# Transposes of q, k and normalised tokens moved from TensorE to the DMA, in a fused window attention and MLP kernel

## The chip, the cores and the metric

One core of one Trainium2 chip. The metric is the device time of one execution in microseconds (us). A kernel is run several times and its median is given; lower is better. Each comparison uses runs of both kernels from the same session on the same chip.

## The reference, cut to what matters

```python
# q, k, v: (4, 8, 768, 64) float32; n_sink = 4, window = 128
scores = q @ k.transpose(0, 1, 3, 2) / sqrt(64)
keep = is_sink | in_window            # 4 sink columns, and the last 128 positions
a = softmax(where(keep, scores, -1e9))
x = heads_merged(a @ v)               # (4, 768, 512)
xn = (x - mean) / sqrt(var + 1e-6) * g_ln
out = x + relu(xn @ w_ch1) @ w_ch2    # 512 -> 2048 -> 512
```

A tile is 128 positions of one batch with all heads: 24 tiles, 6 for each batch. The scores need q and k with the head dimension on the partitions, and the up-projection needs the tokens with the model dimension on the partitions. So both have to be transposed.

## The kernel before

A small planner in the kernel orders the operations: each has a cost on an engine, and the emitted program is the order in which the planner would start them. In the kernel before, TensorE transposes q and k, and VectorE or ScalarE fetch the result out of PSUM:

```python
def prep(b, c, hp, key):              # one head pair of one batch
    ...
    for x in range(2):                # q, k
        for r in range(e):
            for h2 in range(2):
                nc.tensor.transpose(pb.t[64 * h2:64 * (h2 + 1), x, 128 * r:128 * (r + 1)],
                                    qn[(b, x)].t[:, c, 2 * hp + h2, D * r:D * (r + 1)], ident)
    ...                               # copy(eng, kb.t[...], pb.t[...]) on VectorE or ScalarE
```

For each tile the attention result is centred, transposed on TensorE, and fetched with the LN weight:

```python
ENG[e].tensor_scalar(xnb[t].t, xf, mvb[g][:, ti, 0:1], None, op0=ALU.subtract)
...
for j in range(NDM):
    nc.tensor.transpose(pt.t[:, 128 * j:128 * (j + 1)], xnb[t].t[:, 128 * j:128 * (j + 1)], ident)
...
nc.vector.tensor_tensor(xtb[g].t[...], pt.t[...], gt.unsqueeze(2).to_broadcast(...), op=ALU.mult)
```

The attention of batch b+1 is woven into the MLP of batch b, so TensorE always has matmuls to do, as long as the data of batch b+1 is there in time.

Names in the views below: qkn is q and k as loaded, qkt the same transposed; xn is a tile's normalised tokens, xnt the same transposed; vn is v; pm, pw and bank are PSUM buffers. The sink scores are those against the 4 sink columns. A narrow up-matmul is one of 256 columns; the others have 512.

The softmax here doesn't subtract the row's maximum and nothing guards it: scores larger than these inputs give would overflow.

Of the kernel before, what the change touches and what calls it, by code (L numbers as in the profile page):

```python
# [31 lines left out]
class Plan:  # L32
# [4 lines left out]
    LAT = {"PE": 0.2, "ACT": 0.1, "DVE": 0.1, "POOL": 0.15, "DMA": 2.0, "SP": 0.1}  # L37
    SLACK = {"PE": 0.15}
# [15 lines left out]
    def emit(self):  # L54
# [3 lines left out]
        def ready(o):  # L58

            r, held = 0.0, False  # L60
            for d in o.deps:
                if d.end is None:
                    return None, False
                r = max(r, d.end)
            n = {}
            for b in o.alloc:
                h = hist.get(b.pool, [])
                k = n[b.pool] = n.get(b.pool, -1) + 1
                if len(h) + k >= b.bufs:
                    for u in h[k - b.bufs].users:  # L70
                        if u.end is not None:
                            r = max(r, u.end)
                        elif b.pool == "pw":
                            held = True
                        else:
                            return None, False
            return (None if held else r), held

        trace = []
        while waiting:  # L80
# [29 lines left out]
            o.end = s + c + self.LAT[e]  # L110
# [10 lines left out]
def kernel(  # L121
# [12 lines left out]
    nc = tc.nc  # L134
# [67 lines left out]
    LEAD = 24.0  # L202
# [24 lines left out]
    gt = consts.tile([128, NDM], FP32)  # L227
    nc.scalar.dma_start(gt, moe_g_ln.rearrange("(j p) -> p j", p=128))
# [34 lines left out]

    nc.vector.memset(neg_half, -0.5)
# [11 lines left out]
    chunks_of = {b: 2 if b == 0 else 1 for b in range(B)}  # L276

    qn, loaded = {}, {}

    def load_qk(b, c, x, h0, h1, key, deps=()):  # L280
        n = chunks_of[b]
        w = S // n
        alloc = []
        if (b, x) not in qn:
            qn[(b, x)] = Buf("qkn", 4)
            alloc = [qn[(b, x)]]
        qb = qn[(b, x)]

        def go(_):
            if qb.t is None:  # L290
                qb.t = qkn.tile([128, n, H, w // 128 * D], BF16, name="qkn")
            nc.gpsimd.dma_start(qb.t[:, c, h0:h1], (q, k)[x][b, h0:h1, c * w:(c + 1) * w, :]  # L292
                                .rearrange("h (p r) d -> p h (r d)", p=128))

        o = op({"POOL": 0.6 + 0.04 * (h1 - h0)}, go, [begun] + list(deps), key, alloc, [qb])
        o = op({"DMA": (h1 - h0) * w * 256 / 390e3}, None, [o], key)
        for h in range(h0, h1):
            loaded[(b, c, x, h)] = o
        return o
# [3 lines left out]
    def load_v(b, r, key, deps=()):  # L303
        def go(_):
            nc.gpsimd.dma_start(vn_buf[b % 2][:, r, :, 0:D],  # L305
                                v[b, :, 128 * r:128 * (r + 1), :].rearrange("h p d -> p h d"))

        before = [vread[(b - 2, i)] for i in (r, r + 1) if (b - 2, i) in vread] + [vs_done.get(b - 2)]
        o = op({"POOL": 0.9}, go, [begun] + list(deps) + before, key)
        vcast[(b, r)] = op({"DMA": 1.15}, None, [o], key)  # L310
        return o
# [5 lines left out]
    def load_w(which, c, after, key):  # L317
# [8 lines left out]
        o = op({"POOL": 0.9}, go, after, key)  # L326
        w_in[(which, c)] = op({"DMA": 2.65}, None, [o], key)
        return o

    op({"DMA": 1.4}, None, (), -1000)  # L330
    for half in range(2):
        for x in range(2):
            load_qk(0, 0, x, 4 * half, 4 * half + 4, -500 + half)
    for r in range(2):
        load_v(0, r, -486 + r)
    for x in range(2):
        load_qk(0, 1, x, 0, H, -491 + x)
    wi = begun
    w_key = [-460, -452, -450, -448]
    for r in range(2, RB):  # L340
        load_v(0, r, -470 + 5 * r)
    for c in range(4):
        wi = load_w(1, c, [wi], w_key[c])
    for c in range(W2_FIRST):
        wi = load_w(2, c, [wi, w_in.get((1, c))], -440 + c)
    for x in range(2):
        wi = load_qk(1, 0, x, 0, H, -436 + x, [wi, w_in[(1, 2 + x)]])
    for c in range(W2_FIRST, 4):
        wi = load_w(2, c, [wi, w_in[(2, 0)]], -434 + c)
    for r in range(RB):  # L350
        load_v(1, r, -430 + r, [loaded[(1, 0, 0, 0)]])
# [4 lines left out]
    def prep(b, c, hp, key):  # L356

        n = chunks_of[b]
        e = S // (128 * n)
        w = 128 * e  # L360
        alloc = []
        if b not in kqb:
            kqb[b] = Buf("qkt", 2)
            alloc = [kqb[b]]
        kb = kqb[b]
        pb = Buf("pm", 3) if n > 1 else Buf("pw", 2)

        def go(_):
            if kb.t is None:
                kb.t = qkt.tile([128, 2, HP, S], BF16, name="qkt")  # L370
            if n > 1:
                pb.t = ps_m.tile([128, 512], FP32, name="pm").bitcast(BF16)[:, 0:2 * w]
                pb.t = pb.t.rearrange("d (x m) -> d x m", x=2)
            else:
                pb.t = ps_w.tile([128, 2, 512], FP32, name="pw").rearrange("d x m -> d (x m)").bitcast(BF16)
                pb.t = pb.t.rearrange("d (x m) -> d x m", x=2)
            for x in range(2):
                for r in range(e):
                    for h2 in range(2):
                        nc.tensor.transpose(pb.t[64 * h2:64 * (h2 + 1), x, 128 * r:128 * (r + 1)],  # L380
                                            qn[(b, x)].t[:, c, 2 * hp + h2, D * r:D * (r + 1)], ident)

        deps = [ident_done] + [loaded[(b, c, x, h)] for x in range(2) for h in (2 * hp, 2 * hp + 1)]
        o0 = op({"PE": 0.12 * e + 0.2}, go, deps, key, alloc + [pb], [kb] + [qn[(b, x)] for x in range(2)])
        for xs in ([(0, 1)] if n > 1 else [(0,), (1,)]):
            def back(eng, x0=xs[0], x1=xs[-1] + 1):
                copy(eng, kb.t[:, x0:x1, hp, c * w:(c + 1) * w].rearrange("d x (p r) -> d x p r", r=e),
                     pb.t[:, x0:x1, 0:w].rearrange("d x (r p) -> d x p r", r=e))

            m = len(xs) * w  # L390
            o = op({"DVE": 0.18 + m * 0.00101, "ACT": 0.16 + m * 0.00084}, back, [o0], key, (), [pb, kb])
            for x in xs:
                prepped[(b, c, hp, x)] = o

    def ready(b, hps, lo, hi):
        n = chunks_of[b]
        w = S // n
        return [prepped[(b, c, hp, x)] for c in range(n) for hp in hps for x in range(2)
                if c * w < hi and (c + 1) * w > lo]
# [3 lines left out]
    def sinks(b, key):  # L403
# [37 lines left out]
        o1 = op({"DVE": 0.2}, mul_k, ready(b, range(HP), 0, S) + [sunk.get(b - 2), sinks_done], key, (), [kb])  # L441
        ov = op({"PE": 0.22}, mm_v, [vcast[(b, 0)], sinks_done, ones_done], key, [vb])
        vs_done[b] = op({"DVE": 0.7}, mul_v, [ov, vread.get((b - 2, RB - 1))], key, (), [vb])
        o2 = op({"PE": 0.4}, mm, [o1], key, [pb], [kb])
# [4 lines left out]
    def scores(t, halves, key):  # L449
# [32 lines left out]
        o0 = op({"PE": cost}, mm, ready(b, hps, 128 * r, 128 * r + n) + [neg_done, edone.get((t - 1, 1)) if last else None], key, pbs + ebs, [kb])  # L482
# [38 lines left out]
    def values(t, key):  # L521
# [58 lines left out]
        def cen(e):  # L580
            xf = xb[t].t.rearrange("p h d -> p (h d)")
            xnb[t].t = xnpool.tile([128, DM], BF16, name="xn")
            ENG[e].tensor_scalar(xnb[t].t, xf, mvb[g][:, ti, 0:1], None, op0=ALU.subtract)
# [4 lines left out]
        o = op({"DVE": 0.42}, cen, [o], key, [xnb[t]], [xb[t]])  # L588
# [11 lines left out]
        pt = Buf("pt", 1)  # L600
        alloc = [pt]
# [4 lines left out]
        def tr(_):  # L606
            if xtb[g].t is None:
                xtb[g].t = xtpool.tile([128, NDM, 512], BF16, name="xnt")
            pt.t = pt_view
# [3 lines left out]
        def back(_):  # L613
            nc.vector.tensor_tensor(xtb[g].t[:, :, 128 * ti:128 * (ti + 1)],  # L614
                                    pt.t[:, 0:512].rearrange("p (j c) -> p j c", j=NDM),
                                    gt.unsqueeze(2).to_broadcast([128, NDM, 128]), op=ALU.mult)

        o = op({"PE": 0.24}, tr, [o], key, alloc, [xnb[t]] + ([] if ti == 0 else [xtb[g]]))
        turned[t] = op({"DVE": 0.69}, back, [o], key, (), [pt, xtb[g]])
# [33 lines left out]
    def down(g, ti, quarter, key):  # L653
# [18 lines left out]
        if quarter == 3:  # L672
# [13 lines left out]
            op({"DMA": 0.8}, put, [o], -300 + key, (), [ob])  # L686
# [10 lines left out]

    for b in range(B):
        k0 = bkey[b]
        if b == 0:  # L700
            for c in range(2):
                for hp in range(HP):
                    prep(0, c, hp, k0 + (0.6 if c else -40) + 0.1 * hp)
# [17 lines left out]
        if b > 1:  # L721
            for x in range(2):
                load_qk(b, 0, x, 0, H, k0 - 60 + x, [vcast[(b - 1, RB - 1)]])
            for r in range(RB):
                load_v(b, r, k0 - 50 + r, [loaded[(b, 0, 0, 0)]])
        for hp in range(HP):
            prep(b, 0, hp, k0 - 12 + 3 * hp)
# [53 lines left out]
```

## Time and profile before

| | before |
|---|---|
| median of 3 runs | 240.51 us (240.5 to 240.91) |
| span of the profiled run | 239.2 us |
| TensorE busy | 228.8 us (96%) |

The lines on which the prediction rests are in the prediction. Its rows of digits cut the span into 40 equal slices, a digit being the busy share of a slice in tenths (9 is 90% or more). One view is added here. It cuts the run into stretches; the columns are the length, TensorE's busy time (number of instructions), the granted TensorE clock (1 is full), the DMA share (above 1 where the two DMA queues overlap) and GB/s. Kernel before:

```profile
core 0: us, PE busy (x), PEclk, DMA share, GB/s
20.00:50.00 30.00, 29.43 (x328) 1.00 1.51 188
50.00:80.00 30.00, 29.76 (x313) 1.00 0.96 132
80.00:110.00 30.00, 29.35 (x317) 1.00 0.84 98
110.00:140.00 30.00, 29.76 (x290) 1.00 0.10 36
140.00:170.00 30.00, 30.00 (x209) 1.00 0.10 36
```

After 20 us TensorE is never idle for as much as 0.7 us in 30, at full clock.

### The profile page before, as it was taken

What the parts mean: (1) busy time and instruction counts of PE and PEld (TensorE: products, weight loads), DVE (VectorE), ACT (ScalarE), POOL (GpSimd) and SP (SyncE); (2) the same over time, 40 slices, a digit from 0 to 9 for tenths busy, and PEclk for the clock granted to TensorE, in tenths of its full rate; (3) what the DMA queues carried; (4) which work ended last, traced back from release to release, by engine and by line L of the source; (5) the groups of instructions that cost most, each with busy time, mean ns of one, the idle gap of its engine ahead of it and who ended that gap; (6) DMA issues with size and microseconds to landing.
All of it is one profiled execution on the core that took longest, in us unless ns stands there. A gap on an engine that the chain in (4) does not pass through costs nothing.

```text
span 239.2 us, 4785 instructions
## 1 busy us (share of the span) xinstructions
PE 228.8 (96%) x2051; PEld 130.3 (54%) x2051; DVE 119.6 (50%) x231; ACT 121.1 (51%) x193; POOL 59.3 (25%) x86
## 2 busy tenths in 40 slices
PE   7779999999999989999999999999999999999993
PEld 7344788874545654545545544455445455444850
DVE  0247973026798587766766745666204664021002
ACT  2678768865451668862157580706730455500810
POOL 8965448800460922240000200200000211000000
PEclk9999999999999999999999999999999999999999
DMA  6999999999295499200111000211002110001202
GB/s 69 160 182 194 198 207 175 178 188 205 59 162 105 84 202 183 18 3 13 75 47 44 4 0 3 88 44 47 0 1 88 47 44 0 3 22 65 90 0 88
DMA packets 43622, 20.23 MB, mean 85 GB/s; under 512 B 30289, under 2 KB 40529, under 8 KB 43601
## 3 DMA queue, kind: packets, MB, share of 16 engines
q0 software_dynamic: 39616, 13.63, 50.6%
q1 hardware_dynamic: 3456, 6.29, 7.1%
q8 instruction: 16, 0.26, 0.4%
q10 hardware_dynamic: 528, 0.00, 0.1%
q14 instruction: 6, 0.04, 0.1%
HBM read 27.27 MB, written 6.29 MB: 140 GB/s over the span
## 4 chain that ended last, share of the span: by engine, by line
PE 85%; DVE 6%; DMA 4%; POOL 2%; ACT 1%; issue 1%; POOLq 0%
PE pm L665 34%; PE pm L634 34%; PE pw L475 4%; DMA qkn<-in_k_dram 4%; PE pw L380 3%; PE bank L611 3%; PE pw L542 2%; DVE xt L569 2%; POOL qkn L292 2%; PE pw L545 2%; DVE qkt L183 2%; PE pw L535 1%; ACT qkt L181 1%; DVE st L575 1%; PE pw L471 1%
## 5 line engine op out<-in xcount | busy, mean ns | idle before, releaser
L634 PE MATMUL pm<-xnt,w1s 128*128 128x256 bf16 (+1 forms) x512 | 89.9, 326 | 0.0
L486 ACT ACTIVATE e<-pw 128x1024 bf16<-128x1024 f32 x44 | 43.7, 1023 | 49.8 <-PE pw L475 49.6
L634 PEld LDWEIGHTS <-w1s 128*128 128x128 bf16 x512 | 48.0, 98 | 29.6 <-issue 1.5
L665 PE MATMUL pm<-w2s,h1t 128*128 128x512 bf16 x256 | 58.9, 379 | 0.0
L643 ACT ACTIVATE h1t<-pm 128x512 bf16<-128x512 f32 x60 | 35.9, 598 | 25.5 <-PE pm L634 25.1
L678 DVE SCALAR_TENSOR_TENSOR ot<-pm,rs,xt 128x512 f32<-128x512 f32 x24 | 18.0, 750 | 45.7 <-PE pm L665 45.5
L665 PEld LDWEIGHTS <-h1t 128*128 128x128 bf16 x256 | 24.1, 98 | 28.1 <-issue 1.1
L643 ACT ACTIVATE h1n<-pm 128x256 bf16<-128x256 f32 x63 | 24.0, 384 | 18.7 <-PE pm L634 15.8
L665 PE MATMUL pm<-w2s,h1n 128*128 128x512 bf16 x128 | 30.1, 379 | 0.0
L594 POOL TENSOR_SCALAR ve<-mv 128x2 f32<-128x2 f32 (+1 forms) x8 | 2.4, 305 | 82.6 <-DVE mv L578 82.1
L305 POOL DMA_DIRECT2D vn<-in_v_dram x24 | 21.2, 906 | 5.8 <-PE pw L545 4.7
L183 DVE COPY qkt<-pw 128x768 bf16<-128x768 bf16 x10 | 9.6, 958 | 21.6 <-ACT qkt L181 21.2
L614 DVE TENSOR_TENSOR xnt<-bank,gt 128x512 bf16<-128x512 bf16 x24 | 16.4, 685 | 7.5 <-PE bank L611 7.3
L665 PEld LDWEIGHTS <-h1n 128*128 128x128 bf16 x128 | 11.6, 98 | 12.5 <-issue 0.6
L498 POOL TENSOR_SCALAR_AFFINE_SELECT e<-e 128x512 bf16<-128x512 bf16 (+1 forms) x8 | 6.1, 759 | 49.6 <-ACT e L486 49.6
L496 DVE TENSOR_TENSOR e<-e,mask 128x1024 bf16<-128x1024 bf16 x22 | 15.0, 687 | 5.8 <-ACT e L486 5.6
L569 DVE TENSOR_TENSOR xt<-pw,rc 128x512 bf16<-128x512 f32 x24 | 16.6, 691 | 0.8
L575 DVE BATCH_NORM_STATS2 st<-xt 128x6 f32<-128x512 bf16 x24 | 16.5, 690 | 0.5
L380 PEld LDWEIGHTS <-qkn 128*64 128x64 bf16 x384 | 11.4, 109 | 8.9 <-issue 3.6
L542 PE MATMUL pw<-vn,e 128*128 128x65 bf16 x192 | 15.8, 193 | 0.0
L542 PEld LDWEIGHTS <-e 128*128 128x128 bf16 x192 | 13.7, 98 | 2.7 <-DMA vn<-in_v_dram 0.2
L475 PE MATMUL pw<-qkt 64*128 64x256 bf16 (+1 forms) x192 | 14.8, 263 | 0.2 <-DVE qkt L183 0.2
(55 smaller groups left out, 179.4 us busy)
## 6 DMA issues: line engine op xcount, KB each, us to landing
out_dram<-ot SPq DMA_DIRECT2D x24, 256.0 KB, 2.0
vn<-in_v_dram POOLq DMA_DIRECT2D x24, 128.0 KB, 8.2
qkn<-in_q_dram POOLq DMA_DIRECT2D x3, 768.0 KB, 10.9
qkn<-in_k_dram POOLq DMA_DIRECT2D x3, 768.0 KB, 12.4
w1s<-in_moe_w_ch_dram POOLq DMA_DIRECT2D x4, 512.0 KB, 11.7
w2s<-in_moe_w_ch_dram POOLq DMA_DIRECT2D x4, 512.0 KB, 11.4
qkn<-in_q_dram POOLq DMA_DIRECT2D x2, 192.0 KB, 4.5
qkn<-in_k_dram POOLq DMA_DIRECT2D x2, 192.0 KB, 4.6
```

What stands on the lines that cost most here:

```text
L305: nc.gpsimd.dma_start(vn_buf[b % 2][:, r, :, 0:D], v[b, :, 128 * r:128 * (r + 1), :].rearrange("h p d -> p h d"))
L380: nc.tensor.transpose(pb.t[64 * h2:64 * (h2 + 1), x, 128 * r:128 * (r + 1)], qn[(b, x)].t[:, c, 2 * hp + h2, D * r:D * (r + 1)], ident)
L475: nc.tensor.matmul(pb.t[:, h2, i], lhsT=kb.t[64 * h2:64 * (h2 + 1), 1, hp, 128 * r:128 * (r + 1)], rhs=kb.t[64 * h2:64 * (h2 + 1), 0, hp, ...
L486: nc.scalar.activation(eb.t, pb.t, AF.Exp, scale=scale)
L542: nc.tensor.matmul(pv[:, half, hh, :], lhsT=weights_of(t, half, i, h2, 0), rhs=vn[:, r, h, 0:D + 1], start=fresh and hh == 0, stop=(r == 0 ...
L569: nc.vector.tensor_tensor(xb[t].t.rearrange("p (a h) d -> p a h d", a=2), pv[:, :, :, 0:D], rc[0].unsqueeze(3).to_broadcast([128, 2, 4, D] ...
L575: nc.vector.bn_stats(st, xf)
L614: nc.vector.tensor_tensor(xtb[g].t[:, :, 128 * ti:128 * (ti + 1)], pt.t[:, 0:512].rearrange("p (j c) -> p j c", j=NDM), gt.unsqueeze(2).to ...
L634: nc.tensor.matmul(pb.t[:, 0:n], lhsT=w1s[:, j, 128 * ht:128 * (ht + 1)], rhs=xtb[g].t[:, j, 0:n], start=(j == 0), stop=(j == NDM - 1))
L643: nc.scalar.activation(hb.t[:, 0:n], pb.t[:, 0:n], AF.Relu)
L665: nc.tensor.matmul(pb.t, lhsT=h1b[(g, ht)].t[:, 128 * ti:128 * (ti + 1)], rhs=w2s[:, ht, :], start=(ht == 0), stop=(ht == NH1 - 1))
L678: nc.vector.scalar_tensor_tensor(ob.t, in0=pb.t, scalar=rsb[g][:, ti:ti + 1], in1=xb[t].t.rearrange("p h d -> p (h d)"), op0=ALU.mult, op1 ...
```

## The change

The intent: take the transposes off the engine that is the bound. q and k of batches 1 to 3 come in small loads (128 positions, all heads) and each is turned by one DMA transpose issued by SyncE. The tokens of batches 1 to 3 are turned by a DMA transpose too. The call for such a transpose takes no weight, so the LN weight goes into the centring, as one VectorE instruction with two operations ("the fold" below). Core of the diff, cuts marked:

```diff
-                        nc.tensor.transpose(pb.t[64 * h2:64 * (h2 + 1), x, 128 * r:128 * (r + 1)],
-                                            qn[(b, x)].t[:, c, 2 * hp + h2, D * r:D * (r + 1)], ident)
...
+            nc.gpsimd.dma_start(dst[:, r], (q, k)[x][b, :, 128 * r:128 * (r + 1), :].rearrange("h p d -> p h d"))
...
+            nc.sync.dma_start_transpose(kb.t[:, x, :, 128 * r:128 * (r + 1)], qb.t[:, H * D * r:H * D * (r + 1)])
+        o = op({"SP": 0.75}, go, [lo], key, alloc, [kb, qb])
+        prepped[(b, r, x)] = op({"XD": 0.7}, None, [o], key, (), [kb, qb])
...
-            ENG[e].tensor_scalar(xnb[t].t, xf, mvb[g][:, ti, 0:1], None, op0=ALU.subtract)
+            nc.vector.scalar_tensor_tensor(xnb[t].t, in0=xf, scalar=mvb[g][:, ti, 0:1], in1=gb,
+                                           op0=ALU.subtract, op1=ALU.mult)
...
+        if b > 0:
+            o = op({"SP": 0.75}, lambda _: nc.sync.dma_start_transpose(room(), xnb[t].t), [o], key, alloc, ...)
+            turned[t] = op({"XD": 0.7}, None, [o], key, (), [xnb[t], xtb[g]])
+            return
```

The two `op` lines: the planner takes a transpose to cost SyncE 0.75 us and to land 0.7 + 2.0 us after that, on a resource "XD" of its own. The rest of the diff spreads the LN weight over the partitions with one matmul, limits the loads in flight to seven, puts the loads in another order, and changes some planner settings (slack per engine; the lead of a batch's attention, 24 to 30).

## The prediction

> **What bounds the kernel now**
>
> I read the page first (busy times, slices), then the chain in order of time, then short windows of the DMA.
>
> ```profile
> PE 228.8 (96%) x2051; PEld 130.3 (54%) x2051; DVE 119.6 (50%) x231; ACT 121.1 (51%) x193; POOL 59.3 (25%) x86
> ...
> PE   7779999999999989999999999999999999999993
> ...
> DMA  6999999999295499200111000211002110001202
> ...
> PE 85%; DVE 6%; DMA 4%; POOL 2%; ACT 1%; issue 1%; POOLq 0%
> ```
>
> TensorE is busy 96% of 239.2 us and makes up 85% of the chain; VectorE and ScalarE stand at half. A busy TensorE need not be at its peak, so I look at the chain in order of time:
>
> ```profile
> 37.81 12.31 PE pm L634 x112
> 50.13 0.79 PE pw L380 x24
> 50.92 0.97 PE pm L665 x4
> 51.89 0.81 PE pw L380 x24
> ...
> 67.58 0.33 PE bank L611 x4
> 67.91 1.73 PE pm L665 x8
> 69.64 0.22 PE bank L611 x4
> ...
> 228.14 6.92 PE pm L665 x32
> 235.09 0.75 DVE ot L678
> ```
>
> Eight 512-column matmuls take 1.73 us, 216 ns each, in an unbroken stream: the MLP is at its rate, and each instruction among it costs its own time. The reader sees what the q/k transposes (24 per head pair) cost there, 0.79 to 0.86 us a group, and what the four token transposes of a tile cost, 0.22 us (0.33 us in some places). Four matmuls after a q/k group take 0.97 us in place of 0.86. So whatever leaves TensorE after about 15 us should shorten the run, unless a wait takes its place. TensorE's idle time there is small: from the windows 50 to 80, 80 to 122 and 122 to 166 us, 30 - 29.76, 42 - 41.35 and 44 - 43.76, together 1.1 us, mostly at the q/k transposes, whose results VectorE and ScalarE have to fetch out of PSUM.
>
> The other resource that is full is DMA, up to about 60 us: its row reads 9 for nine slices, at 160 to 207 GB/s. Small-row loads run slower than large-row ones:
>
> ```profile
> 92.00:93.00 1.00, 1.00 (x10) 0.53 (x9) 0.07 (x1) 1.00 (x2) 0.00 (x0) 1.00 2.50 152
> ```
>
> ```profile
> vn<-in_v_dram POOLq DMA_DIRECT2D x24, 128.0 KB, 8.2
> out_dram<-ot SPq DMA_DIRECT2D x24, 256.0 KB, 2.0
> ```
>
> The window is a microsecond with only v loads (last column GB/s): 152, so a 128 KB load takes some 0.85 us. In the page's DMA issues the last column is issue to landing; the last line's is a store's, 2.0 us in the median.
>
> **What the Trainium skill says**
>
> - VectorE: DVE Perf Modes, section "The three transpose paths": a 128x128 bf16 transpose takes 390 ns on TensorE and 1309 ns through the DMA crossbar, which lands in SBUF. Those are single times; in this trace four on TensorE occupy 0.22 us, because they are pipelined. No run before has the DMA path.
> - DMA: Bandwidth & Descriptors, section "Latency and other measured facts": the DMA transpose was measured at 261 GB/s, about 350 to 400 if contiguous. A 128x512 bf16 tile is 131 KB, so I estimate 0.5 us of transfer for each. This trace can't confirm it.
> - The same page, "Issuing engines are not separate DMA queues": all issuers share 16 DMA engines and interleave. The trace agrees: a store lands in 2.0 us alone, but in up to 5.8 us (the tile view's longest) while loads are in flight.
> - TensorEngine Tiling (Array Packing), section "Key Properties": changing the tiling mode drains TensorE. That agrees with 0.97 for 0.86 us after a group that writes 64-wide column tiles: 0.11 us for each such group.
>
> **The change part by part**
>
> *Removed from TensorE.* Batches 1 to 3 have 4 head pairs each, 12 groups of 24 transposes: 12 x 0.81 = 9.7 us. Their mode switches: 12 x 0.11 = 1.3 us. The token transposes of 18 tiles: 18 x 0.22 = 4.0 us. The idle gaps that the fetches out of PSUM and the LN chain made between 50 and 166 us: up to 1.1 us. All of it lies in the stretch in which TensorE is the bound. Sum 16.1 us.
>
> *Removed from the other engines.* 14 fetches on ScalarE (799 ns) and 10 on VectorE (958 ns), 11.2 and 9.6 us; and 24 weighted fetches of tokens on VectorE, 685 ns, 16.4 us. Six plain copies stay for batch 0, five of them on ScalarE in the new order. Off the path, worth nothing by itself; it only leaves VectorE more slack.
>
> *Added.* The centring becomes a scalar_tensor_tensor with the weight: 402 ns become some 750 (the output's instruction of that kind and size took 750), 24 x 0.35 = 8.4 us on VectorE, less than the 26 it loses. One fp32 matmul that spreads the LN weight, before the first q/k has landed (14.7 us for the last of batch 0), so hidden.
>
> *DMA.* 54 transposes on SyncE's queue, 54 x 0.5 = 27 us of DMA time by the estimate. The q and k loads of batches 1 to 3 become 36 loads of 128 KB in the form of v's: 12 x 0.85 = 10.2 us a batch, against 1.57 MB at about 205 GB/s = 7.7 us. From 60 us on, DMA is mostly idle and this is hidden. In the first 60 us it is not.
>
> *Where it can bite: batch 1.* In the new instruction order the first scores of batch 1 stand after 120 of the 192 narrow up-matmuls of batch 0; before, its q/k transposes stood after all 192 (at 50.13 us). 72 x 0.108 us = 7.8 us earlier: TensorE gets there at about 42.4 us. Loads ahead of it are 6.0 MB, and slices 1 to 6 of the page carry (69 + 160 + 182 + 194 + 198 + 207) x 5.98 us = 6.0 MB, so they end at about 36 us; the trace has the third w2 load landing at 37.6. The scores need three small loads: 37.6 + 3 x 0.85 = 40.2, then a transpose of 2 us alone, up to 4 beside loads: 42 to 44 us. A stall of 0 to 2 us. Next the sink scores of batch 1, about 13 us of TensorE work later by the counts in the order and the times above, at 55.5 to 56 us. They need all of q: the fifteenth small load, one w2 load of 2.6 us and ten transposes before it: 37.6 + 15 x 0.85 + 2.6 + 10 x 0.5 = 58, plus 2 us to land = 60 us. A stall of some 4 us, which contains the first one. TensorE runs in order and nothing after makes it good.
>
> *Later batches* are loaded right behind batch 1, long before their scores (80 us and 120 us). Tokens have time too: the shortest way from the last values of a group to its first up-matmul is about 11 us of TensorE work in the new order, against some 2.5 us on VectorE and 3 to 5 for the transfer.
>
> Sum: 240.5 - 16.1 + 4.0 = 228.4 us.
>
> **Rivals**
>
> 1. *All hidden.* The transposes are short and land before TensorE asks: 240.5 - 16.1 = 224.4. For it: the loads and transposes are issued in small pieces, and the planner's modelled latencies are generous. Against it: DMA is already full when batch 1 is wanted, and the order brings it forward by 8 us.
> 2. *DMA transposes are far slower than a copy.* If each 128x128 block took the page's single 1309 ns in turn, 54 x 4 x 1.3 = 281 us would be more than the whole run, and DMA would become the bound, at 280 us or more. Against it: 16 engines share the work, the same skill gives 261 GB/s[...]. At half the estimated rate (1 us each) the batch 1 stall grows by 5 us: 233.
> 3. *SyncE's queue blocks.* It is in order and mixes q/k transposes, token transposes and stores. In the new order a token transpose of the first tile of batch 1 stands before the last two q/k transposes of that batch: it waits for scores, values and LN of that tile, at about 53 us. That is earlier than q's last load, so it should add nothing; if the scores slip by 4 us, it slips too and could add 1 to 3 us: 230 to 231.
> 4. *VectorE becomes the bound.* Against it: it is busy 50% now and loses more than it gains.
>
> **Range and chances**
>
> Between no stall (224.4) and a stall of 10 us (234), with a little for a better start (less VectorE work for each tile of batch 0): 223.5 to 234, and 228.4 as the middle. Faster by over 2% means under 235.7; that needs under 11.3 us of new stalls. 0.90 for it. Within 2%: 0.06. Slower: 0.04, which is rival 2.
>
> **What will show it**
>
> TensorE's busy time should fall by about 15 us to 213 or 214; the groups of q/k transposes should keep only batch 0 (96 matmuls) and the token transposes only 24. The waits of TensorE should name the DMA of the transposed q/k at batch 1, once or twice, some 4 us in all between 42 and 62 us, and nearly none after. The DMA view should show transposes landing in 2 to 3 us when loads are quiet and in 4 us or more before 60 us. I am wrong if TensorE waits for transposed q/k in batches 2 and 3 or for transposed tokens, if transposes take over 1 us of DMA time each, if SyncE's order holds up batch 1 longer than its loads do, or if TensorE's busy time falls by much less than 15 us.

## The result

| | before | after |
|---|---|---|
| median | 240.71 us (240.5 to 244.23, 4 runs) | 249.65 us (248.44 to 250.01, 4 runs) |
| ratio of fast runs | 1 | 1.0366, 95% interval 1.032 to 1.0411 |
| span of the profiled run | 239.2 us | 248.3 us |
| mean granted clock | 1.000 | 0.950 |

Ratios here and below are the mean time of one kernel's fast runs over that of the other's fast runs of the same rounds, so not quite the ratio of the medians that are quoted (before's 244.23, over 1.5% above its fastest, is not in it). The change made the kernel 3.7% slower; 228.4 us was predicted. The results are correct.

The page of the kernel after, the lines that answer to those shown of before:

```profile
PE 222.6 (90%) x1670; PEld 121.5 (49%) x1690; DVE 109.3 (44%) x207; ACT 110.8 (45%) x178; POOL 87.9 (35%) x115
...
PE   6978999379749999839999999999999999999993
...
PEclk9979999959968999968999999999999999999999
DMA  6999999999992999999947990122101231012102
...
PE 71%; DMA 19%; POOL 3%; DVE 2%; SPq 1%; issue 1%; ACT 0%; POOLq 0%; DVEq 0%
```

TensorE's row has three holes (slices 8, 12 and 18, of 6.2 us each), where it had none. The clock row dips at or behind each hole. DMA, which before had little to do from slice 17 on, is busy to slice 24 but for slices 13, 21 and 22, and makes 19% of the chain that ends last, where it made 4%. The same stretches as above, kernel after:

```profile
20.00:50.00 30.00, 24.43 (x282) 0.99 1.66 177
50.00:80.00 30.00, 24.00 (x181) 0.78 1.54 137
80.00:110.00 30.00, 24.77 (x207) 0.96 1.63 161
110.00:140.00 30.00, 29.84 (x200) 0.93 1.31 129
140.00:170.00 30.00, 29.78 (x205) 1.00 0.67 94
```

From 140 us on both kernels are alike. All is lost before. What TensorE waited for, kernel after (us in total, times, longest):

```profile
PE pm L446 <- DMA qkt<-qkn: 9.7, 2, 4.9
PE pw L487 <- DMA qkt<-qkn: 5.1, 1, 5.1
```

And where, from the timeline of the kernel after (start, length, what, and in brackets the idle time before it):

```profile
50.98 1.04 PE L487 MATMUL pw<-qkt 64*128 64x256 bf16 x8 [5.07 <-DMA qkt<-qkn]
...
71.62 0.62 PE L446 MATMUL pm<-qkt,ks 128*32 128x512 bf16 x4 [4.82 <-DMA qkt<-qkn]
72.17 4.74 PE L686 MATMUL pm<-w2s,h1n 128*128 128x512 bf16 x11
...
109.58 0.62 PE L446 MATMUL pm<-qkt,ks 128*32 128x512 bf16 x4 [4.91 <-DMA qkt<-qkn]
```

The first is the first scores of batch 1, the second its sink scores (which need all of q), the last the sink scores of batch 2. Together 5.07 + 4.82 + 4.91 = 14.8 us. The third line shows what follows a wait: eleven 512-column matmuls in 4.74 us, some 430 ns each, where 216 was the rate. The clock records say the same; the stretches of half clock in the kernel after, with TensorE's busy time in them:

```profile
15.20:18.60 3.40, 3.14 (x32) 0.50 1.57 192
49.33:56.16 6.83, 5.18 (x28) 0.50 1.93 151
69.81:76.64 6.83, 5.02 (x15) 0.50 0.90 147
107.36:114.18 6.82, 4.60 (x20) 0.50 1.99 156
```

Half of that busy time is lost: 17.9 / 2 = 9.0 us. (The first stretch lies in the start-up and occurs in some of the profiled runs here and not in others.) With this the books close. Work taken off TensorE, at full clock: 228.8 - (222.6 - 9.0) = 15.2 us. Idle time: 248.3 - 222.6 = 25.7 us, where before had 239.2 - 228.8 = 10.4, so 15.3 us more. 239.2 - 15.2 + 15.3 + 9.0 = 248.3. These are books, not yet causes: a part of them that is taken away may come back elsewhere, and the experiments show that it does.

Why did the transposes come late? Kernel after, the tile view of the transposed q and k: first the issue on SyncE (shortest, median and longest in ns), then the us from issue to landing:

```profile
L399 SPq DMA_TRANSPOSE qkt<-qkn x36: 1189/1252/3184, 38.6 to 146.0; - x36
...
DMA to landing us min/median/max: 2.4/7.4/9.4
```

A transpose lands 2.4 us after its issue when DMA is quiet and 7 to 9 us after it beside loads. It keeps SyncE for 1.25 us in the median, not 0.75. What one costs the DMA itself shows in a window with one token transpose alone (154 to 158 us), beside one with a store of 256 KB alone (226 to 230 us):

```profile
154.00:158.00 4.00, 4.00 (x26) 1.00 0.16 33
226.00:230.00 4.00, 4.00 (x20) 1.00 0.17 66
```

0.16 x 4 = 0.64 us for 33 x 4 = 132 KB: 206 GB/s. A transposed byte costs the DMA nearly twice what a stored one does (0.17 x 4 = 0.68 us for 264 KB).

Batch 2 was late for a further reason. GpSimd issues the loads, in order, and it stood at the window mask of a tile whose scores waited for batch 1. GpSimd's timeline, kernel after:

```profile
79.50 0.64 POOL L510 TENSOR_SCALAR_AFFINE_SELECT e<-e 128x512 bf16<-128x512 bf16 x1 [17.07 <-ACT e L498]
```

DMA worked off what was in flight until some 74 us and was nearly idle for the last 6 of these 17 us (slice 13 of its row, 2), and the loads of batch 2's later tiles came out at 81 us and after. Whether this made the third wait is tested in experiment 4. The last q transpose that its sink scores need was issued at 101.8 us and landed at 109.5.

### The profile page after: what moved, and what is told of

Read it like the earlier page. It is cut to its first block, busy times and chain, and to the rows that moved or that the text cites. A ratio compares the mean times of both kernels' runs of the same rounds, so it can differ in the third digit from the quotient of the medians.

```text
span 248.3 us, 4183 instructions
## 1 busy us (share of the span) xinstructions
PE 222.6 (90%) x1670; PEld 121.5 (49%) x1690; DVE 109.3 (44%) x207; ACT 110.8 (45%) x178; POOL 87.9 (35%) x115
## 3 DMA queue, kind: packets, MB, share of 16 engines
q0 software_dynamic: 70816, 13.64, 67.5%
## 4 chain that ended last, share of the span: by engine, by line
PE 71%; DMA 19%; POOL 3%; DVE 2%; SPq 1%; issue 1%; ACT 0%; POOLq 0%; DVEq 0%
PE pm L686 33%; PE pm L655 29%; DMA qkt<-qkn 10%; DMA qkn<-in_q_dram 5%; PE pw L487 4%; DMA qkn<-in_k_dram 4%; PE pw L554 2%; POOL qkn L310 2%; PE pw L557 1%; SPq L399 1%; PE pw L547 1%; PE pm L446 1%; DVE xt L581 1%; DVE st L587 1%; PE pw L483 0%
## 5 line engine op out<-in xcount | busy, mean ns | idle before, releaser
L655 PE MATMUL pm<-xnt,w1s 128*128 128x256 bf16 (+1 forms) x505 | 91.1, 334 | 0.4
L655 PEld LDWEIGHTS <-w1s 128*128 128x128 bf16 x512 | 50.1, 101 | 35.6 <-issue 4.5
L686 PE MATMUL pm<-w2s,h1t 128*128 128x512 bf16 x249 | 56.9, 379 | 0.4
L699 DVE SCALAR_TENSOR_TENSOR ot<-pm,rs,xt 128x512 f32<-128x512 f32 x24 | 18.0, 749 | 68.1 <-PE pm L686 50.9
L664 ACT ACTIVATE h1n<-pm 128x256 bf16<-128x256 f32 x56 | 20.9, 386 | 20.0 <-PE pm L655 17.7
L510 POOL TENSOR_SCALAR_AFFINE_SELECT e<-e 128x512 bf16<-128x512 bf16 (+1 forms) x7 | 4.9, 704 | 63.8 <-ACT e L498 63.8
L607 POOL TENSOR_SCALAR ve<-mv 128x2 f32<-128x2 f32 (+1 forms) x8 | 5.3, 668 | 38.8 <-DVE mv L590 38.6
L508 DVE TENSOR_TENSOR e<-e,mask 128x1024 bf16<-128x1024 bf16 x23 | 16.4, 720 | 5.5 <-ACT e L498 5.2
L595 DVE SCALAR_TENSOR_TENSOR xn<-xt,mv,gb 128x512 bf16<-128x512 bf16 x24 | 18.3, 767 | 0.8
L325 POOL DMA_DIRECT2D qkn<-in_k_dram x18 | 16.1, 895 | 6.0 <-DMA w2s<-in_moe_w_ch_dram 1.9
L325 POOL DMA_DIRECT2D qkn<-in_q_dram x18 | 16.4, 908 | 1.1 <-PE pm L655 0.5
```

What stands on the lines that cost most here:

```text
L325: nc.gpsimd.dma_start(dst[:, r], (q, k)[x][b, :, 128 * r:128 * (r + 1), :].rearrange("h p d -> p h d"))
L595: nc.vector.scalar_tensor_tensor(xnb[t].t, in0=xf, scalar=mvb[g][:, ti, 0:1], in1=gb, op0=ALU.subtract, op1=ALU.mult)
L655: nc.tensor.matmul(pb.t[:, 0:n], lhsT=w1s[:, j, 128 * ht:128 * (ht + 1)], rhs=xtb[g].t[:, j, 0:n], start=(j == 0), stop=(j == NDM - 1))
L664: nc.scalar.activation(hb.t[:, 0:n], pb.t[:, 0:n], AF.Relu)
L686: nc.tensor.matmul(pb.t, lhsT=h1b[(g, ht)].t[:, 128 * ti:128 * (ti + 1)], rhs=w2s[:, ht, :], start=(ht == 0), stop=(ht == NH1 - 1))
L699: nc.vector.scalar_tensor_tensor(ob.t, in0=pb.t, scalar=rsb[g][:, ti:ti + 1], in1=xb[t].t.rearrange("p h d -> p (h d)"), op0=ALU.mult, op1 ...
```

## The experiments

First theory: three late landings of transposes, made by a DMA that is full, cost the time, and the half clock behind each adds to it. Rivals: the half clock alone makes the loss; the planner's wrong costs made a bad order, which a better order would mend; the parts that seemed harmless (fold of the LN weight, token transposes) cost. All kernels gave correct results. Each line of numbers is the median, the range and the ratio to before of its own session (the medians of before lay between 240.77 and 241.93).

### 1. Spins at the three waits

The kernel after with junk matmuls ahead of the three groups.

```diff
+            for _ in range(getattr(o, "fill", 0)):
+                self.spin()
+        o2.fill = 80 if b in (1, 2) else 0       # sink scores
+        o0.fill = 80 if t in (6,) else 0         # first scores of batch 1
```

> The changed kernel with 80 junk matmuls (about 55 ns each, 4.4 us in all) put on TensorE ahead of each of the three groups at which it stood idle for some 5 us: the first scores of batch 1 and the sink scores of batches 1 and 2. Theory A (TensorE waits for transposed q and k, and each wait of 5 us is followed by some 5 us at half clock because TensorE was idle): the waits stay in length, their half-clock stretches go, 3 x 2.5 = 7.4 us less than 249.65, about 242. Rival B (the half clock comes from the DMA traffic or from power, not from idleness): the half-clock stretches stay, 249 to 250.

Measured: 250.99 us (248.32 to 253.12; two runs fast, 248.32 and 249.41), ratio 1.0332. At batch 1 the spins ran out before q came, 4.4 us of idleness were left, and half clock followed (51.8 to 58.6 us). At the two sink scores only 0.3 and 1.1 us of idleness were left, and no half clock followed. So the half clock follows TensorE's idleness and not the DMA traffic. (The profiled run is one of the two slow ones, 252.56 us: its waits and clock are read here, not its time.) The fast runs are no faster than the kernel after, against what was expected. A reading, which the later runs bear out: the landings set the times, and the work that half clock had slowed had only been slowed ahead of the next wait.

### 2. Parts of the change alone

Four kernels. The tokens alone, on the kernel before, with the fold that they need:

```diff
+        if b > 0:
+            o = op({"SP": 0.75}, lambda _: nc.sync.dma_start_transpose(room(), xnb[t].t), ...)
```

> The kernel before with the LN weight in the centring and the DMA transposes of the normalised tokens past batch 0 alone; q and k stay on TensorE, loads as before. Theory A: no wait of TensorE for a DMA transpose, since tokens have over 10 us of slack; 18 x 0.22 = 4.0 us less than 240.5, plus up to 3.5 us of the start-up loss that the changed kernel showed: 236.5 to 240. Rival C (any DMA transposes in a stream with loads and stores cost more than they save): 241 or more, with waits for xnt.

Measured: 243.76 us (243.05 to 246.39), ratio 1.0139, a miss. TensorE waited 3.8 us once for transposed tokens, at 88 us, and half clock followed for 3.4 us.

q and k alone: the kernel after with all tokens on TensorE.

```diff
-        if b > 0:
+        if False:                                # tokens by DMA
```

> The changed kernel with the tokens of all batches transposed on TensorE again; only q and k go through DMA. Theory A: the loss sits in q and k. The waits stay, the one at the sink scores of batch 1 some 1 to 3 us shorter, because no token transpose stands ahead of the last q in SyncE's queue, TensorE has 4.0 us more to do: 246 to 251. Rival D (the token transposes in SyncE's queue are what holds q and k up): waits of under 2 us each and no half clock, 235 to 238.

Measured: 244.8 us (243.58 to 245.77), ratio 1.015. It waits 6.6 and 2.2 us for q/k at batch 1 and no longer at batch 2. So the token transposes had a part in the third wait; whether by their place in SyncE's queue, by their DMA time or by the order of the plan, this run does not tell.

The fold alone, on the kernel before:

```diff
-            ENG[e].tensor_scalar(xnb[t].t, xf, mvb[g][:, ti, 0:1], None, op0=ALU.subtract)
+            nc.vector.scalar_tensor_tensor(xnb[t].t, in0=xf, scalar=mvb[g][:, ti, 0:1], in1=gb,
+                                           op0=ALU.subtract, op1=ALU.mult)
...
-        turned[t] = op({"DVE": 0.69}, back, ...)                 # with the weight
+        turned[t] = op({"DVE": 0.69, "ACT": 0.59}, back, ...)    # a plain copy, on either engine
```

> The kernel before with the LN weight in the centring alone (fp32 matmul that spreads it, scalar_tensor_tensor, plain copies of the tokens): no DMA transposes. If the start-up loss of 3.5 us comes with this part (TensorE starts its warm-up matmuls 3 us later, behind the fp32 matmul that waits for the weight): 243 to 244. If it comes from the new order of loads or from the planner's other numbers: 240 to 241.

Measured: 244.22 us (244.04 to 245.04), ratio 1.0145, at full clock. A part that was counted as free costs 3.4 us by the medians. In the same session the fold with the token transposes took 243.76 us, so moving the tokens on top of the fold gains nothing that shows. To see whether the late spread of the weight was the cause (an fp32 matmul that waits 2.4 us for its load in the start-up), the weight was spread by the load itself:

```diff
+    nc.scalar.dma_start(gb, moe_g_ln.rearrange("(o d) -> o d", o=1).broadcast_to([128, DM]))
```

> The LN weight in the centring alone, as in e4_fold (244.2), but spread by its load: no fp32 matmul ahead of the warm-up. If the late warm-up was the cause of e4_fold's 3.4 us: 240.5 to 241.5. If it is the longer centring on VectorE and the copies that went to ScalarE: 243 to 245.

Measured: 245.43 us (244.21 to 246.62), ratio 1.0162: it was not. The fold comes back in experiment 6.

### 3. The order: a planner told the measured costs

The kernel after with the same instructions; only the planner's costs of a transpose differ ("the honest plan" below).

```diff
-    LAT = {..., "DMA": 2.0, "XD": 2.0, "SP": 0.1}
+    LAT = {..., "DMA": 2.0, "XD": 5.0, "SP": 0.1}
-        o = op({"SP": 0.75}, go, [lo], key, alloc, [kb, qb])
-        prepped[(b, r, x)] = op({"XD": 0.7}, None, [o], key, (), [kb, qb])
+        o = op({"SP": 1.25}, go, [lo], key, alloc, [kb, qb])
+        o = op({"DMA": 0.8}, None, [o], key - 400)
+        prepped[(b, r, x)] = op({"XD": 0.0}, None, [o], key, (), [kb, qb])
...                                              # the same for the tokens
```

> The changed kernel with the same instructions, only in another order: the planner is told what the trace of the changed kernel measured of DMA transposes (1.25 us to issue, 0.8 us taken from the same DMA engines as the loads, 5 us more until they have landed), so it puts more MLP work ahead of the scores of batch 1 and 2. Theory A (the loss is TensorE's in-order wait for transposes that land later than planned): the three waits fall from 14.8 us to under 3 and the half-clock stretches go with them; the start-up loss stays: 228 to 233. Rival C (DMA transposes are too expensive in themselves, whatever the order): the waits move elsewhere, 240 or more.

Measured: 241.9 us (240.51 to 245.89), ratio 1.0006, interval 0.9938 to 1.0074. So with nothing but the order changed, the loss against before is gone: 7.7 us by the medians of the two sessions. But 228 to 233 us was a miss. The waits at batch 1 are gone, and others are there at 81 to 96 us, when the MLP of batch 0 is used up. Timeline of this kernel:

```profile
83.97 0.61 PE L488 MATMUL pw<-qkt 64*128 64x256 bf16 x4 [2.53 <-DMA qkt<-qkn]
...
91.09 0.40 PE L555 MATMUL pw<-vn,e 128*128 128x65 bf16 x4 [1.93 <-DVE e L503]
...
95.69 0.59 PE L657 MATMUL pm<-xnt,w1s 128*128 128x512 bf16 x1 [2.54 <-issue]
```

No wait is longer than 2.54 us, and still the clock is halved for 17.07 us (83.5 to 100.6). The same kernel, the stretch from 80 to 110 us:

```profile
80.00:110.00 30.00, 20.58 (x129) 0.72 1.82 161
```

Is that half clock a cost? The same kernel with 150 junk matmuls ahead of the four groups that waited:

```diff
+        o0.fill = {12: 45, 13: 20}.get(t, 0)              # scores of batch 2
+        o.fill = {12: 40}.get(t, 0)                       # values of batch 2
+        o.fill = 45 if (g, ht) == (3, 0) else 0           # first up-matmuls of the fourth group
```

> The kernel with the honest plan (all DMA transposes, LN fold; 241.9 us), with 150 junk matmuls ahead of the four groups that waited between 81 and 97 us, where TensorE ran at half clock for 17 us after small waits. Theory: idleness alone halves the clock and half of that stretch is lost work: no half clock between 83 and 101 us, and 233 to 236 us. Rival: transposes and VectorE set the times there as in the run with spins ahead of the three long waits: clock full, but 240 to 243 us.

Measured: 241.75 us (240.58 to 242.7), ratio 0.9993. The clock is full but for one stretch of 3.4 us, and the time is the same: the rival holds. The same stretch in this kernel:

```profile
80.00:110.00 30.00, 27.11 (x284) 0.94 1.80 153
```

The DMA share is as it was (1.82 and 1.80). What TensorE does here waits for the data, at whatever clock.

### 4. GpSimd's mask and the start-up

The kernel after with all window masks on VectorE, so that GpSimd can't stand at one ahead of loads:

```diff
-                    o = op({"POOL": 1.28, "DVE": 0.69}, window, [o, masks_done], key, (), [eb])
+                    o = op({"DVE": 0.69}, window, [o, masks_done], key, (), [eb])
```

> The changed kernel with all window masks on VectorE; none is left on GpSimd. In the changed kernel GpSimd stood 17 us at one mask, ahead of the loads of q, k and v of batch 2 for the tiles from the third on. Theory A, second part (the third wait, at the sink scores of batch 2, comes from loads that stand behind that mask in GpSimd's queue): that wait of 4.9 us and its half clock of some 2.3 us go, 241 to 244, and the two waits in batch 1 stay. Rival: the loads then collide with those of batch 1 and with its transposes, and the first waits grow by as much: 247 to 252.

Measured: 250.8 us (249.37 to 251.71), ratio 1.0389. It waits 7.0, 3.8 and 5.9 us for q/k. The third wait stayed, and grew from 4.9 to 5.9 us with no gap in the DMA's row before it, so the mask was not what made it, or not alone; that part of the theory fell. What made batch 2's transposes late stays open between the DMA's load, SyncE's queue and the order.

The kernel after with the weight spread by its load (the edit of the second fold kernel):

> The changed kernel with the LN weight spread over the partitions by its load, not by an fp32 matmul, so that TensorE starts its warm-up matmuls 3 us earlier, as before. If the start-up loss (3.7 us at the 64th narrow up-matmul) comes from the late warm-up (half clock from 15.2 to 18.6 us): 1.5 to 3.5 us are gained before the first wait. But if the first wait's end is set by the landing of the transposes alone, the gain is swallowed by it: then the run stays within 1 us of 249.65 and the first wait is longer by what the start-up gained.

Measured: 249.25 us (248.5 to 251.07), ratio 1.0341. It tells little: in its trace the half clock of the start-up is still there (16.3 to 19.7 us), and TensorE stands at the first scores of batch 1 only 0.5 us sooner (45.4 us, 45.9 in the kernel after). Experiment 6 has a run that does gain time at the start. All three together (planner, masks, load):

> The three edits together: planner told of the measured transposes, masks on VectorE alone, LN weight spread by its load. Theory A: no wait of TensorE over 2 us, no half clock after 10 us, 16 us less TensorE work than before: 225 to 230. Rival C: 238 or more.

Measured: 243.14 us (242.35 to 244.28), ratio 1.0089, a miss. None of the orders and start-ups tried here brings all of this change under before.

### 5. Only where DMA has room

The kernel before with only q and k of batches 2 and 3 by DMA, with the measured costs in the planner. No fold, tokens and batch 1 on TensorE.

```diff
+        if b >= 2:
+            return [prepped[(b, r, x)] for x in range(2) for r in range(RB) if ...]
...
+            for r in range(RB):
+                for x in range(2):
+                    load_qk_rows(b, x, r, k0 - 60 + r, ...)      # small load, then DMA transpose
-        for hp in range(HP):
-            prep(b, 0, hp, k0 - 12 + 3 * hp)
+        if b < 2:
+            for hp in range(HP):
+                prep(b, 0, hp, k0 - 12 + 3 * hp)
```

> The kernel before, its LN weight and its token transposes as they were, with DMA transposes for q and k of batches 2 and 3 alone: batch 1 keeps its large-row loads and its TensorE transposes. Theory A (DMA transposes pay where the DMA engines have room and the scores are far off): 8 of the 12 groups leave TensorE, 8 x 0.92 = 7.4 us and some 0.9 us of idle gaps; no wait for qkt over 1 us and no half clock: 231 to 235. Rival C (they cost more than they save wherever they stand): 239 or more.

Measured: 236.12 us (235.06 to 238.01), ratio 0.9786, interval 0.9723 to 0.9849. It is faster than before, clear of noise (by 2% or by a little less, the interval does not say), and TensorE never waits for a transposed q or k. Its stretches:

```profile
50.00:80.00 30.00, 29.50 (x295) 1.00 2.00 168
80.00:110.00 30.00, 27.97 (x245) 1.00 1.55 148
```

With the tokens of batches 2 and 3 by DMA as well; the fold is in these tiles only, and the weight is spread by a load:

```diff
+        if b >= 2:
+            o = op({"SP": 1.25}, turn, [o], key, alloc, [xnb[t], xtb[g]])    # nc.sync.dma_start_transpose
+            ...
+            return
```

> The run before this one with DMA transposes for the tokens of batches 2 and 3 too, the weight in the centring for those tiles alone (its spread copy loaded late, behind v of batch 1). Theory A: another 12 x 0.22 = 2.6 us, without the start-up loss: 228.5 to 232.5. Rival: tokens stand behind q and k or stores in SyncE's queue and TensorE waits for xnt: no gain or a loss against the run before this one.

Measured: 235.82 us (235.19 to 236.02), ratio 0.976: no gain that the intervals show, where 12 x 0.22 = 2.6 us of transposes are gone. No wait for tokens is in its trace. In the profiled run TensorE stands idle for 2.0 us between 184 and 186.3 us, for VectorE and for GpSimd's mask, with 3.4 us of half clock behind it, where the run before has neither; whether the other runs have it is not known.

A control: the kernel before with q and k of batches 1 to 3 in the small loads, still transposed on TensorE.

```diff
+            dst = qb.t.rearrange("p (r h d) -> p r h d", r=RB, h=H)
+            nc.gpsimd.dma_start(dst[:, r], (q, k)[x][b, :, 128 * r:128 * (r + 1), :].rearrange("h p d -> p h d"))
```

> The kernel before with q and k of batches 1 to 3 loaded in 128 KB pieces with short rows, as the change does, and still transposed on TensorE. It tells what the form of the loads costs by itself. By the rates of the trace, 2.5 us of DMA a batch, of which only batch 1's can reach TensorE: 241 to 243. If the loads were the main cause of the late batch 1: 245 or more.

Measured: 243.26 us (242.87 to 243.79), ratio 1.008: small loads alone cost about 2 us; its sink scores of batch 1 start at 65.1 us, before's at 58.2. Part of the full DMA is theirs: the time of the load queue's packets, as a share of the 16 engines' span, is 50.6% before, 68.1% here and 67.5% in the kernel after, for the same bytes.

Batch 1 added to the winner:

```diff
-        if b >= 2:
+        if b >= 1:
             return [prepped[(b, r, x)] for x in range(2) for r in range(RB) if ...]
```

> The kernel with q and k of batches 2 and 3 by DMA (236.1 us), and batch 1 also: no fold, tokens on TensorE. Theory: batch 1 is what costs, since its transposes share a DMA that is full until its scores are due: waits for transposed q/k between 44 and 75 us, and 240 to 245 us, in spite of 4 groups of transposes (3.7 us with their switches) less on TensorE. Rival: the fold and the tokens cost, batch 1 does not: 232 to 234 us and no wait over 1.5 us for transposed q/k.

Measured: 238.12 us (233.89 to 238.88), one run fast and three over 1.5% above it, so no interval. It was run again, unchanged:

> Batches 1 to 3 of q and k by DMA, no fold, tokens on TensorE, unchanged: its four runs lay between 233.9 and 238.9 and three were called slow by the rule of 1.5% above the fastest. The question is whether batch 1 adds to the gain of batches 2 and 3 (236.1 us): if its transposes are hidden, a median of 232 to 235; if what TensorE saves is given back where DMA is full, 236 to 239.

Measured: 236.44 us (236.15 to 237.43, 5 runs), ratio 0.9827, interval 0.9794 to 0.9859. So batch 1 does not make the kernel slower, as the first theory had it, and gains nothing that shows over batches 2 and 3. The stretches of this kernel:

```profile
50.00:80.00 30.00, 27.46 (x221) 1.00 1.83 157
80.00:110.00 30.00, 24.75 (x209) 1.00 2.08 156
```

The 12 groups take 9.7 + 1.3 = 11.0 us off TensorE by the prediction's own terms, which would be 240.8 - 11.0 = 229.8 us. It is 6.6 us above that, and here they are: 2.5 + 5.3 = 7.8 us idle in these two stretches, where before has 0.24 + 0.65 = 0.9. The waits are not for q and k but for a w2 load (2.1 us at 58.6), for v (2.1 us at 93.6) and for VectorE (2.0 us at 80.7). The transposes push the other loads back: v's loads land 17.0 us after their issue in the median, against 5.1 us in the control with the same small loads and no DMA transposes. Why VectorE is late was not looked into.

### 6. What the fold and the tokens cost

The fold alone, with the token copies kept on VectorE:

```diff
-        turned[t] = op({"DVE": 0.69, "ACT": 0.59}, back, [o], key, (), [pt, xtb[g]])
+        turned[t] = op({"DVE": 0.69}, back, [o], key, (), [pt, xtb[g]])
```

> The kernel before with the LN weight in the centring, the copies of the transposed tokens kept on VectorE. If the 3.4 us that the fold cost come from the copies that moved to ScalarE: 240.5 to 242. If they come from the centring that went from 402 to some 767 ns in the chain that leads to a group's tokens: 243.5 to 246.

Measured: 241.89 us (241.56 to 242.09) where before had 240.84, ratio 1.0 (0.9917 to 1.0083). Most of the fold's cost came with the copies on ScalarE, or with the order that the planner made of them; these two were not told apart. The same edit in the kernel after:

> The kernel after, with the six copies of batch 0's transposed tokens all on VectorE (five were on ScalarE); TensorE's order is the same but for a few narrow up-matmuls and four down matmuls. If those copies cost here what they seem to cost in the fold alone (some 2 us at the start): 247 to 248. If the three later landings of transposes set the times, whatever the start does: 249 to 251.

Measured: 249.18 us (248.95 to 250.57), ratio 1.0355: there it makes no difference, since the landings set the times. Its trace shows it: TensorE stands at the first scores of batch 1 2.4 us sooner than in the kernel after (43.5 us against 45.9), waits 8.4 us in place of 5.1, and starts them no sooner (51.95 us against 50.98). In the kernel with the honest plan:

> The kernel with the honest plan (241.9 us) with the copies of batch 0's tokens on VectorE. It then differs from q and k of batches 1 to 3 by DMA alone only by the DMA transposes of tokens and the longer centring. If these two cost nothing: 237 to 239.5. If the token transposes, which stand in the same queue and share the DMA that is full until some 120 us, cost the difference: 241 to 243.

Measured: 241.67 us (240.52 to 243.43), ratio 1.0046. That is 5.2 us above batches 1 to 3 of q and k alone (236.44 us, same session). The two kernels differ by the token transposes and the longer centring, and, which the expectation left out, by the change's order of the loads, its planner settings and the fp32 matmul that spreads the weight (2.4 us of waiting in the start-up); these were not separated further. Where the time goes is plain: the stretch from 80 to 110 us of this kernel has 9.2 us of idle time, and its longest wait is for transposed tokens.

```profile
80.00:110.00 30.00, 20.85 (x130) 0.77 1.83 166
```

```profile
PE pm L657 <- DMA xnt<-xn: 3.5, 1, 3.5
```

## Why the prediction was wrong

**Removed from TensorE (16.1 us): right.** 15.2 us by the books above. q/k transposes and token transposes are left for batch 0 only. The busy time that was to fall to 213 or 214 us reads 222.6, because half clock stretches it; at full clock it is 213.6.

**"A stall of some 4 us" at batch 1: this step failed, by size and by number.** It took a transpose to land in "2 us alone, up to 4 beside loads", from a store's landing. Alone it was right, 2.4 us. Beside loads it is 6.8 to 9.4 us in batch 1. The loads themselves were nearly on time: the third small load landed at 41.2 us (40.2 predicted) and its transpose was issued at 41.5, but landed only at 50.85. So the first scores of batch 1 ran at 50.98 us, not at 42 to 44. (TensorE stood ready for them at 45.9 us, not 42.4: the start-up, which had been counted as hidden, was slower too, but experiment 6 shows that this cost nothing here.) "Which contains the first one" failed too: there were two waits, 5.07 and 4.82 us. The estimate of 0.5 us of DMA time was low but not the main fault: 0.64 us alone. For batch 1's loads, which landed between 37.7 and 65 us, an estimate: 12 x 0.85 + 6 x 0.85 + 2.6 = 17.9 us by the durations in the prediction, so 27.3 - 17.9 = 9.4 us for the 9 transposes that had landed by then and parts of 3 more under way, some 0.8 to 1.0 us each.

**"Later batches are loaded right behind batch 1": failed.** The last transpose for batch 2's sinks was issued at 101.8 us and landed at 109.5, a third wait of 4.91 us, which the prediction had named as a sign of being wrong. That GpSimd stood at a mask did not make it, or not alone (experiment 4); without token transposes it is gone, and with the order of experiment 3 the longest wait for q and k is 2.5 us. Three waits of 14.8 us stand where the sum had 4.0.

**Half clock: not in the sum at all.** The Trainium skill, TensorE: Matmul & The Clock Gate, section "HAM oscillation — how this bites in real kernels", gives the rule: no idle gaps of TensorE above some 3.4 us, or the clock is halved. The trace agrees in the main: in each wait of 4.8 to 5.1 us the clock falls to 0.5, 2.7 to 3.4 us after TensorE stopped, and stays there for 6.83 us. But whoever adds it as a cost overcounts. Two experiments took much of the half clock away, and neither became faster, since what TensorE waited for came no sooner.

**"Tokens have time too": right in the kernel after, not in others.** Its list of waits has none for transposed tokens; but TensorE has other waits there that give them time. It waited 3.8 us for them where they were moved alone and 3.5 us with the honest plan, and in batches 2 and 3, without such a wait, moving them gained nothing that shows.

**"Off the path" for the LN fold: wrong in part.** Alone it costs 3.4 us with copies that may go to ScalarE and about 1 us (by the medians, inside the interval) with copies on VectorE.

**Rivals.** Rival 1 (all hidden) is out by the waits, rival 4 (VectorE) because VectorE's busy time fell from 119.6 to 109.3 us. Rival 2 (281 us of serial transposes) is out by far. Rival 3, SyncE's queue, was seen and put at 1 to 3 us: the last q load of batch 1 had landed at 60.8 us, its transpose was issued only at 64.0, behind a token transpose, and landed at 71.5, which set the second wait. The mechanism was right and its size was right; it lay on top of landings twice as long. "Slower" had a chance of 0.04, and for rival 2 alone; the way in which it came about was on no list.

So where did the 16 us go? By the medians, the first across two sessions: 7.7 us of the loss come back with a planner that knows the true costs (249.65 to 241.9). A further 5.2 us come back without the tokens, the fold, and the order of loads and planner settings that came with them (241.67 to 236.44). What remains short of the sum, 6.6 us, (240.8 - 11.0 = 229.8 us for q and k alone), are waits in a kernel whose DMA stays full to some 130 us, two of the three longest for loads pushed back behind 36 transposes. Only what fits beside that is gained: two batches or three give the same 236 us.

## What to carry to other kernels

Work moved from the bound engine to the DMA was free here only where the DMA had room until the result was wanted, so count the DMA's load over time, not over the whole run, and take the landing time from a trace with the same traffic. Where a planner sets the order, measure the cost of a new instruction before believing the order; and where TensorE waits for data, neither a full clock nor an earlier start helped in these runs. Move only the part that has room: here two batches of q and k gained 2.1%, all of it together lost 3.7%.

## What the Trainium skill lacked or had wrong

- DMA: Bandwidth & Descriptors, "Latency and other measured facts", gives 261 GB/s for the DMA transpose, measured on one kernel; alone in this trace it was 206 GB/s (132 KB in 0.64 us).
- The same page has no landing time of a transpose beside other traffic: 2.4 us alone, 7.4 us in the median of 36, and 9.4 us at most beside loads. For the time that a transpose keeps the issuing engine's queue it has sequencer cycles of "previous generations" in a table on a newer chip, and none for a transpose of this size: 1.19 to 3.18 us here, 1.25 in the median.
- VectorE: DVE Perf Modes, "The three transpose paths", gives 1309 ns for one 128x128; four of them in one instruction took 0.64 us of DMA time here, so the figure can't be multiplied.
- TensorE: Matmul & The Clock Gate, "HAM oscillation — how this bites in real kernels", speaks of gaps above 3.4 us. In the kernel with the honest plan no wait was above 2.54 us, and a run of them gave 17.07 us of half clock. (The page does say further down that frequent short idle times can have this effect, but not how short or how many.)
